# Retention by chunks from block 4 instead of block 8, with values and state as two products in quadrants

## The chip, the cores and the metric

The kernel runs on one core of a Trainium2 chip. The metric is the device time of one execution in microseconds (us), the median over repeated runs. The engines are PE (TensorE, matrix products), DVE (VectorE), ACT (ScalarE), POOL (GpSimd) and SP (SyncE, which here only issues DMAs). Each has its own queue of instructions and works through it in order. They wait for one another through semaphores.

## The reference

The first half is a retention layer, attention without a softmax, in which the weight of a key falls by a factor gamma for each position. The second half is a feed-forward layer with a maximum of three products.

```python
batch, n_heads, seq, head_dim = (8, 8, 576, 64)
scores = scale * np.matmul(q, k.transpose(0, 1, 3, 2))
gamma = 1.0 - 2.0 ** (-5.0 - np.arange(H))
Dmat = np.where(rel >= 0, gamma[:, None, None] ** rel[None, :, :], 0.0)   # rel = query - key
attn = np.matmul(scores * Dmat[None], v)                                  # (8, 8, 576, 64)
x = attn.transpose(0, 2, 1, 3).reshape(4608, 512)
h = np.maximum(np.maximum(x @ w1, x @ w2), x @ w3)                        # w1, w2, w3: 512 x 768
out = h @ w_out                                                           # w_out: 768 x 512
```

q, k and v are fp32. The four weight matrices arrive as float64, and the chip has to turn them into fp32 itself.

## The kernel before

**Tiling.** The 8 x 576 positions are one row of 36 blocks of 128 (`C`), numbered `g`. A sequence is 4.5 blocks long, so it may begin in the middle of a block. `half(c)` is the upper or lower 64 partitions of a tile, and `place(g, c)` says which of the nine half blocks of its sequence a half block is. Nine stages `t` of four blocks each (512 positions, `NT`) go through the feed-forward layer.

**Retention.** The sum over earlier keys is carried as a state, a 64 x 64 matrix for each head: keys (transposed) times values. Blocks 0 to 7 (`g < BY_CHUNKS`) use whole blocks: `transposes` turns keys and queries with PE, and ACT copies them out of PSUM; `scores` multiplies them to 128 x 128 for each head, and DVE multiplies by a causal mask; `state` makes keys times values of the block; `keep` adds it to the state on DVE, and POOL multiplies it by the decay of a block; `values` multiplies values by scores and state by queries; `output` moves the sum into `xT` on DVE, times the query's decay `gq`. In these blocks the values are multiplied by the keys' decay `gk` (POOL, `decay`). Some blocks hold the start of a sequence and use a mask of their own.

From block 8 on, half blocks are used. `chunk_scores` makes, for each head, two score products of 64 x 64 and up to two state products of 64 x 64, on the four quadrants of PE. The tiles `va0` and `va1` hold values in one half of the partitions and the state in the other, and `m0` and `m1` hold masked scores in one half and queries in the other. `chunk_values` then needs one product of full height (128 rows, 64 columns) for each half block and head. For this the queries are copied once on ACT (L313), each half is masked by its own DVE instruction with a mask times key decay, `gm` (L325), and states of a sequence's start are filled with zeros on POOL (L262). The decay `gk` is multiplied into the keys.

**Transposes.** Up to block 6 (`g < BY_PE`) PE transposes. From block 7 on, `load_blocks` brings keys and queries in pieces of 32 x 32, in many small DMAs, and DVE transposes each piece.

**Weights.** `convert_all` makes fp32 out of the float64 words, with DVE and ACT in turn. It works on pairs of 128 rows (`Two`). The first two pairs are done in halves of 512 columns, so that the first half is ready early, all others as 1024 columns at once. `load_weights` issues the next load when a pair is done.

**Feed-forward.** In stage 0 (`up_plain`, `downs_plain`) each of nine units (three pairs of rows times w1, w2, w3) is two times four matmuls of 512 columns, followed by a copy or a maximum (`maximum`). From stage 1 on, `up` and `downs` use products of smaller matrices with sums made beforehand (L766, L564), which needs fewer products.

**The order of the work** is written out by hand. `steps(t)` lists what retention does before each of twelve steps of the previous stage. In stage 0 a step is one unit, and the line `convert(4 if (fp, i) == units[0] else 2)` says how many steps of conversion follow each half unit. DVE's small steps wait in the lists `urgent` and `chores` from stage 1 on and are put between the products; `scaling` is the same for ACT's multiplications by `gk`.

Of the kernel before, what the change touches and what calls it, by code (L numbers as in the profile page):

```python
# [40 lines left out]
FP32 = mybir.dt.float32  # L41
# [11 lines left out]
BY_CHUNKS = 8  # L53
# [28 lines left out]
def kernel(  # L82
# [50 lines left out]
    gq = const.tile([P, 2, NP // 2, C], FP32, name="gq")  # L133
    gm = const.tile([P, H, D], FP32, name="gm")
# [9 lines left out]
                            base=0, channel_multiplier=-1, pattern=[[1, C]])  # L144

# [11 lines left out]
    masks = {0: causal, None: causal}  # L157
    for r in sorted({start_of(g) for g in range(BY_CHUNKS)} - {0, None}):
        m = masks[r] = raw0.tile([C, C], FP32, name=f"causal{r}")
        nc.gpsimd.tensor_copy(m[:], causal[:])  # L160
        nc.gpsimd.memset(m[0:r, r:C], 0.0)


    raws, vds, qks, sts, states, kvs, vas, ms = {}, {}, {}, {}, {}, {}, {}, {}
# [35 lines left out]
    def load_blocks(g, *blocks):  # L200
        for n, src in (("q", q), ("kx", k)):

            if 0 in blocks:
                shape = [P, NP, C // 32, 32] if g < BY_CHUNKS else [P, H, D // 32, 32]
                raws[n, g] = raw.tile(shape, FP32, tag=n, name=n + "raw", bufs=2)
            t = raws[n, g]
            for blk in blocks:
                b, pos = divmod(g * C + 32 * blk, S)
                if g < BY_CHUNKS:
                    for a in range(4):  # L210
                        nc.sync.dma_start(
                            t[32 * a:32 * a + 32, :, blk, :],
                            src[b, a // 2::2, pos:pos + 32, 32 * (a % 2):32 * (a % 2) + 32].rearrange("p j i -> j p i"))
                    continue
                c, e = divmod(blk, 2)
                for a in range(2):
                    r = D * (1 - c) + 32 * a
                    nc.sync.dma_start(
                        t[r:r + 32, :, e, :],
                        src[b, :, pos:pos + 32, 32 * a:32 * a + 32].rearrange("h p i -> p h i"))  # L220

    def stacked(g, c):

        if (g, c) not in vas:
            vas[g, c] = vpool.tile([P, H, D], FP32, tag=f"va{c}", name=f"va{c}")
        return vas[g, c]

    def load(g):
        if g >= BY_PE and ("q", g) not in raws:
            load_blocks(g, *range(C // 32))  # L230
        for n, src in (("k", k), ("q", q), ("v", v)) if g < BY_PE else (("k", k), ("v", v)):
            if n == "v" and g == CPT - 1:
                load_weights(1)
            if n == "v" and g >= BY_CHUNKS:
                for c in range(2):
                    b, pos = divmod(g * C + D * c, S)
                    nc.sync.dma_start(stacked(g, c)[half(c)], v[b, :, pos:pos + D, :].rearrange("h p d -> p h d"))
                continue
            bufs = {"k": 3, "q": 2, "v": 4}[n]
            pool, bufs = (raw0, 1) if n != "v" and g < BY_PE and g % (bufs + 1) == bufs else (raw, bufs)  # L240
            if n == "v":
                t = vpool.tile([C, H, D], FP32, tag="va0", name="vraw")
            else:
                t = pool.tile([C, H, D], FP32, tag=n, name=n + "raw", bufs=bufs)
# [4 lines left out]
    def decay(g):  # L249
        factor = gk[:].unsqueeze(2).to_broadcast([C, H, D])  # L250
        if g < BY_CHUNKS:
            t = vds[g] = vpool.tile([C, H, D], FP32, tag="va1", name="vd")
            nc.gpsimd.tensor_tensor(t[:], raws.pop(("v", g))[:], factor, op=ALU.mult)
            return
        kr = raws["k", g]
        if spread:
            scaling.extend(partial(nc.scalar.mul, kr[:, h, :], kr[:, h, :], gk[:, h:h + 1]) for h in range(H))
        else:
            nc.gpsimd.tensor_tensor(kr[:], kr[:], factor, op=ALU.mult)
        for c in range(2):  # L260
            if place(g, c) == 0:
                nc.gpsimd.memset(vas[g, c][half(1 - c)], 0.0)  # L262
# [4 lines left out]
    def transposes(g):  # L267
        both = qks[g] = {}
        if g >= BY_CHUNKS:
            for n, tag in (("k", "kT"), ("q", "m1")):  # L270
                both[n] = att.tile([P, H, D], FP32, tag=tag, name=tag, bufs=2 if n == "k" else 3)
            ms[g, 1] = both["q"]
        else:
            both["k"] = att.tile([P, NP, C], FP32, tag="kT", name="kT", bufs=2)
            both["q"] = ppool.tile([P, NP, C], FP32, tag="part", name="qT")
        if g >= BY_PE:
# [3 lines left out]
            return  # L280
        for n, src in (("k", raws["k", g]), ("q", raws.pop(("q", g)))):
            pool, tag = (ps_r, "r") if g >= CPT else (ps_x, "x")
            pt = pool.tile([P, NP, C], FP32, tag=tag, name=n + "t")
            for p in range(NP):
                nc.tensor.transpose(pt[:, p, :], pair(src, p), ident[:C, :C])
            nc.scalar.copy(both[n][:], pt[:])

    def scores(g):
# [11 lines left out]
        for j in range(2):  # L300
            st = sts[g, j] = att.tile([C, NP, C], FP32, tag=f"m{j}", name="st", bufs=2 + j)
            soon(partial(nc.vector.tensor_tensor, st[:], s[j][:],
                         masks[start_of(g)][:].unsqueeze(1).to_broadcast([C, NP, C]), op=ALU.mult))

    def begins(g):
        return g + 1 < NG and start_of(g + 1) != 0

    def chunk_scores(g):

        kT, kr = qks[g]["k"], raws.pop(("k", g))  # L310
        sk = [ps_r.tile([P, H, D], FP32, tag="r", name=f"sk{j}") for j in range(2)]
        ms[g, 0] = att.tile([P, H, D], FP32, tag="m0", name="m0", bufs=2)
        nc.scalar.copy(ms[g, 0][half(1)], ms[g, 1][half(1)])  # L313
        for h in range(H):
            for c in range(2):
                if place(g, c) < S // D - 1:
                    nc.tensor.matmul(sk[c][half(c), h, :], lhsT=kr[half(c), h, :], rhs=vas[g, c][half(c), h, :],  # L317
                                     start=True, stop=True)
            for c in (1, 0):
                r = half(1 - c)  # L320
                nc.tensor.matmul(sk[1 - c][half(c), h, :], lhsT=kT[r, h, :], rhs=ms[g, 1][r, h, :],  # L321
                                 start=True, stop=True)

        def mask(c):
            nc.vector.tensor_tensor(ms[g, c][half(c)], sk[1 - c][half(c)], gm[half(c)], op=ALU.mult)  # L325

        def keep_chunk(c):

            to = stacked(g + c, 1 - c)
            if place(g, c) == 0:  # L330
                nc.vector.tensor_copy(to[half(c)], sk[c][half(c)])  # L331
            else:
                nc.vector.tensor_tensor(to[half(c)], sk[c][half(c)], vas[g, c][half(1 - c)], op=ALU.add)  # L333
            if c:
                nc.gpsimd.tensor_tensor(to[half(1)], to[half(1)],  # L335
                                        gs_of[half(1)].unsqueeze(2).to_broadcast([D, H, D]), op=ALU.mult)

        for c in range(2):
            soon(partial(mask, c))
        for c in range(2):  # L340
            if place(g, c) < S // D - 1:
                soon(partial(keep_chunk, c))

    def carry(g):

        for j in range(2):
            nc.scalar.copy(stacked(g, 0)[half(1), j::2, :], states[g][half(j)])

    def state_factors():
        for j in range(2):  # L350
            nc.scalar.copy(gs_of[half(1), j::2], gs[half(j)])

    def key_masks():
        for c in range(2):
            nc.gpsimd.tensor_tensor(gm[half(c)], causal[half(c), half(c)].unsqueeze(1).to_broadcast([D, H, D]),
                                    gk[half(c)].unsqueeze(2).to_broadcast([D, H, D]), op=ALU.mult)

    def state(g):

        kr = raws["k", g]  # L360
        kvs[g] = None
        if begins(g):
            r = start_of(g) or 0
            kvs[g] = ps_r.tile([P, NP, D], FP32, tag="r", name="kv")
            for h in range(H):
                nc.tensor.matmul(kvs[g][half(h % 2), h // 2, :], lhsT=kr[r:, h, :], rhs=vds[g][r:, h, :],
                                 start=True, stop=True)

    def keep(g):
        factor = gs[:].unsqueeze(2).to_broadcast([P, NP, D])  # L370

        def step(t, kv):
            if start_of(g) is not None:
                nc.vector.tensor_tensor(t[:], kv[:], factor, op=ALU.mult)
            else:
                nc.vector.tensor_tensor(t[:], kv[:], states[g][:], op=ALU.add)
                nc.gpsimd.tensor_tensor(t[:], t[:], factor, op=ALU.mult)

        if begins(g):
            t = states[g + 1] = ppool.tile([P, NP, D], FP32, tag="part", name="state")  # L380
            soon(partial(step, t, kvs[g]))
# [7 lines left out]
    def values(chunks, new_states=(), later=False):  # L389

        def before(g):
            return C if start_of(g) is None else start_of(g)

# [5 lines left out]
        pool, tag = (ps_r, "r") if chunks[0] >= CPT - 1 else (ps_y, "y")  # L401
        o = [pool.tile([P, len(chunks), NP // 2, C], FP32, tag=tag, name="o") for _ in range(2)]
        for m, g in enumerate(chunks):
            for n in range(NP):
                for c in range(2):
                    h = head(c, n)
                    nc.tensor.matmul(o[n % 2][half(c), m, n // 2, :], lhsT=vds[g][:, h, :],
                                     rhs=sts[g, h % 2][:, h // 2, :], start=m == 0 and n < 2,
# [604 lines left out]
```

## Time and profile before

| | |
|---|---|
| median of 3 runs | 757.49 us (756.05 to 758.63) |
| profiled run | 756.22 us, span 754.5 us |
| PE matmuls up (L766) | 18% + 15% + 8% + 5% + 5% of the chain that ended last |
| score and state products by chunks (L321, L317) | 896 and 784 records, 220 ns each |
| value products by chunks (L438) | 896 records, 224 ns each |
| masks by chunks on DVE (L325) | 56 of 687 ns, 38.5 us in all |
| copy of the queries on ACT (L313) | 28 of 613 ns, 16.0 us in all |
| multiplication by `gk` on ACT (L186) | 208 of 346 ns, 65.6 us in all |

The profile shows one execution. Busy time is the time in which an engine had at least one instruction in flight; a group's mean is the duration of one instruction, and since matmuls overlap, it isn't what one of them costs. The cost of a stream of matmuls is read from the starts: when the next group of instructions begins. A line is given with the number that it has in this kernel.

### The profile page before, as it was taken

The numbers are of one execution on the slowest core, as the hardware profiler recorded it, in microseconds if no ns is written. First come the engines' busy times: TensorE is split into PE (matmuls) and PEld (weight loads), VectorE is DVE, ScalarE is ACT, GpSimd is POOL, SyncE is SP. The second block draws the span as 40 slices with busy tenths as digits, with TensorE's granted clock in tenths as the row PEclk, the third lists the DMA queues.
The fourth block names the chain that finished last, engine by engine and source line by source line (L and its number), as shares of the span: only waits on it lengthen the run. The fifth ranks groups of instructions, "written<-read, shape, count | busy, mean of one in ns | idle before, by whom it ended". The sixth has DMA issues, their size and how long they took to land.

```text
span 754.5 us, 15014 instructions
## 1 busy us (share of the span) xinstructions
PE 745.1 (99%) x5928; PEld 607.9 (81%) x5928; DVE 529.2 (70%) x879; ACT 336.3 (45%) x670; POOL 90.9 (12%) x112
## 2 busy tenths in 40 slices
PE   8999999999999999999999999999999999999998
PEld 7645545588888888888888888888888888888887
DVE  2998796958886866687567847685768666863662
ACT  3665531155245533553355435542555255414441
POOL 3210012002010110011010102010101010100000
PEclk9999999999999999999999999999999999999999
DMA  9995762504242414242343225242425141000001
GB/s 211 229 244 121 201 140 68 102 1 75 67 101 41 85 43 102 54 74 54 71 85 65 62 60 95 38 77 63 82 40 98 43 91 37 1 30 28 2 1 56
DMA packets 230310, 59.20 MB, mean 78 GB/s; under 512 B 211168, under 2 KB 228960, under 8 KB 230240
## 3 DMA queue, kind: packets, MB, share of 16 engines
q1 hardware_dynamic: 229664, 57.91, 35.5%
q8 instruction: 46, 0.75, 0.4%
q10 hardware_dynamic: 576, 0.33, 0.2%
q14 instruction: 24, 0.20, 0.1%
HBM read 48.76 MB, written 9.44 MB: 77 GB/s over the span
## 4 chain that ended last, share of the span: by engine, by line
PE 89%; DVE 5%; DMA 3%; SPq 1%; issue 1%; ACT 1%; DVEq 0%
PE a L766 18%; PE b L766 15%; PE dx L564 11%; PE c L766 8%; PE up L790 6%; PE dz L564 5%; PE d L766 5%; PE e L766 5%; PE o L438 4%; PE sk L317 3%; PE dy L564 3%; PE down L777 2%; DMA bits<-in_moe_w_out_dram 1%; PE sk L321 1%; SPq L247 1%
## 5 line engine op out<-in xcount | busy, mean ns | idle before, releaser
L754 DVE TENSOR_TENSOR part<-part 128x512 f32<-128x512 f32 x161 | 111.4, 692 | 93.6 <-ACT part L751 91.2
L751 ACT COPY part<-b 128x512 f32<-128x512 f32 x115 | 67.3, 585 | 140.2 <-PE b L766 140.2
L754 DVE TENSOR_TENSOR h<-h,part 128x512 f32<-128x512 f32 x115 | 79.6, 692 | 28.8 <-ACT h L751 24.6
L790 PE MATMUL up<-xT,w 128*128 128x512 f32 (+2 forms) x200 | 84.8, 579 | 1.0 <-DVE w L663 0.9
L751 ACT COPY part<-a 128x512 f32<-128x512 f32 x92 | 53.9, 585 | 48.9 <-PE a L766 48.4
L790 PEld LDWEIGHTS up<-xT,w 128*128 128x128 f32 x200 | 36.8, 190 | 43.3 <-issue 40.1
L766 PE MATMUL a<-s,w 128*128 128x256 f32 x276 | 70.9, 379 | 0.0
L766 PE MATMUL b<-s,n 128*128 128x256 f32 x276 | 70.8, 379 | 0.0
L186 ACT ACTIVATE kraw<-kraw,gk 128x64 f32<-128x64 f32 x208 | 65.6, 346 | 3.2 <-DMA kraw<-in_k_dram 2.9
L766 PEld LDWEIGHTS b<-s,n 128*128 128x128 f32 x276 | 52.4, 190 | 7.1
L766 PEld LDWEIGHTS a<-s,w 128*128 128x128 f32 x276 | 52.4, 190 | 7.2
L534 POOL TENSOR_TENSOR H<-h 128x256 f32<-128x256 f32 x24 | 20.2, 842 | 285.6 <-DVE h L754 285.5
L335 POOL TENSOR_TENSOR va<-va,gs_of 64x512 f32<-64x512 f32 x24 | 25.8, 1074 | 229.8 <-DVE va L333 184.2
L766 PE MATMUL c<-xT,w 128*128 128x256 f32 x184 | 49.1, 389 | 0.0
L766 PE MATMUL d<-s,w 128*128 128x256 f32 x184 | 47.3, 379 | 0.0
L766 PE MATMUL b<-xT,n 128*128 128x256 f32 x184 | 47.2, 379 | 0.0
L564 PE MATMUL dx<-To,H 128*128 128x256 f32 (+1 forms) x204 | 44.9, 370 | 0.0
L766 PE MATMUL e<-xT,w 128*128 128x256 f32 x184 | 43.5, 379 | 0.0
L766 PE MATMUL a<-xT,n 128*128 128x256 f32 x184 | 43.5, 379 | 0.0
L564 PEld LDWEIGHTS dx<-To,H 128*128 128x128 f32 x204 | 36.6, 190 | 4.9
L325 DVE TENSOR_TENSOR m<-sk,gm 64x512 f32<-64x512 f32 x56 | 38.5, 687 | 1.0
L766 PEld LDWEIGHTS e<-xT,w 128*128 128x128 f32 x184 | 35.0, 190 | 5.2 <-DVE va L331 0.2
(122 smaller groups left out, 1318.1 us busy)
## 6 DMA issues: line engine op xcount, KB each, us to landing
bits<-in_moe_w_dram SPq DMA_DIRECT2D x36, 256.0 KB, 5.5
out_dram<-osb SPq DMA_DIRECT2D x35, 256.0 KB, 2.1
kraw<-in_k_dram SPq DMA_DIRECT2D x32, 256.0 KB, 3.1
qraw<-in_q_dram SPq DMA_DIRECT2D x224, 32.0 KB, 2.2
kxraw<-in_k_dram SPq DMA_DIRECT2D x224, 32.0 KB, 2.1
va<-in_v_dram SPq DMA_DIRECT2D x56, 128.0 KB, 3.1
bits<-in_moe_w_out_dram SPq DMA_DIRECT2D x6, 512.0 KB, 6.3
vraw<-in_v_dram SPq DMA_DIRECT2D x7, 256.0 KB, 4.5
```

The source lines that it names most:

```text
L186: scaling.popleft()()
L317: nc.tensor.matmul(sk[c][half(c), h, :], lhsT=kr[half(c), h, :], rhs=vas[g, c][half(c), h, :], start=True, stop=True)
L325: nc.vector.tensor_tensor(ms[g, c][half(c)], sk[1 - c][half(c)], gm[half(c)], op=ALU.mult)
L335: nc.gpsimd.tensor_tensor(to[half(1)], to[half(1)], gs_of[half(1)].unsqueeze(2).to_broadcast([D, H, D]), op=ALU.mult)
L438: nc.tensor.matmul(o[half(c), n % 2, n // 2, half(m)], lhsT=vas[g, m][:, h, :], rhs=ms[g, m][:, h, :], start=m == 0 and n == 0, stop=True, ...
L534: urgent.append(lambda: (pool(s3, a11, a21, op=ALU.subtract), pool(s4, a12, s2, op=ALU.subtract)))
L564: nc.tensor.matmul(o, lhsT=hS[n](fp)[:, m * P:(m + 1) * P], rhs=late["T"][n][:, fp, cols], start=first and fp == order[0] and (m == 0 or l ...
L751: nc.scalar.copy(of[step], ps[step[0]][:])
L754: nc.vector.tensor_tensor(of[dst], a, b, op=op)
L766: nc.tensor.matmul(ps[chain][:, e, :], lhsT=factor(w, 2 * fp + e), rhs=xS[t][x], start=n == 1 and e == 0, stop=ends, skip_group_check=True)
L777: nc.tensor.matmul(b[:], lhsT=h[:, fb, m * P:(m + 1) * P], rhs=w_sb["out", fb], start=(fb == 0), stop=(fb == NF - 1))
L790: nc.tensor.matmul(ps[:, cols], lhsT=w_sb[i, fb][:, dc * P:(dc + 1) * P], rhs=xT[t][:, dc, cols], start=dc == 0 and cols.start == 0, stop= ...
```

## The change

`BY_CHUNKS` falls from 8 to 4, so blocks 4 to 7 are done by chunks too. The form of the work by chunks changes:

- `chunk_scores` makes scores (`sk`) and new states (`kv`) in one PSUM tile each, and masks with one DVE instruction for a block.
- Values and state are two products, each on quadrants of 64 x 64: `chunk_values` first multiplies values by masked scores, then the state by the queries, into the same two PSUM tiles for two blocks. For the first half block of a sequence the second product is left out.
- The decay `gk` is multiplied into the values, no longer into the keys. The mask `low` is then only ones and zeros.
- Values are loaded as a whole block. States have tiles of their own (`stacks`).
- `transposes` for blocks 4 to 6 puts PE's result in the layout by chunks with eight ACT copies of 64 partitions in place of two of 128.
- Gone are the tiles `gm` and `m0`'s copy of the queries, the zero fills, and the masks for blocks in which a sequence starts.
- In the conversion the third pair of weights is done in halves too. In stage 0 the second unit gets as many conversion steps as the first, and for the last unit the maximum is put ahead of the conversion.

```diff
-BY_CHUNKS = 8
+BY_CHUNKS = 4
...
     def decay(g):
         factor = gk[:].unsqueeze(2).to_broadcast([C, H, D])
...
+        t = raws.pop(("v", g))
+        if spread:
+            vds[g] = t
+            scaling.extend(partial(nc.scalar.mul, t[:, h, :], t[:, h, :], gk[:, h:h + 1]) for h in range(H))
             return
...
+        vds[g] = t if g >= BY_CHUNKS else vpool.tile([C, H, D], FP32, tag="s", name="vd")
+        nc.gpsimd.tensor_tensor(vds[g][:], t[:], factor, op=ALU.mult)
...
     def transposes(g):
...
+        if g >= BY_CHUNKS:
+            for n, pt in pts:
+                for j in range(2):
+                    for c in range(2):
+                        nc.scalar.copy(both[n][half(c), j::2, :], pt[half(j), :, half(c)])
...
     def chunk_scores(g):
...
-        sk = [ps_r.tile([P, H, D], FP32, tag="r", name=f"sk{j}") for j in range(2)]
-        ms[g, 0] = att.tile([P, H, D], FP32, tag="m0", name="m0", bufs=2)
-        nc.scalar.copy(ms[g, 0][half(1)], ms[g, 1][half(1)])
+        s, kv = (ps_r.tile([P, H, D], FP32, tag="r", name=n) for n in ("sk", "kv"))
+        kept = [c for c in range(2) if place(g, c) < S // D - 1]
         for h in range(H):
             for c in range(2):
-                if place(g, c) < S // D - 1:
-                    nc.tensor.matmul(sk[c][half(c), h, :], lhsT=kr[half(c), h, :], rhs=vas[g, c][half(c), h, :],
-                                     start=True, stop=True)
-            for c in (1, 0):
-                r = half(1 - c)
-                nc.tensor.matmul(sk[1 - c][half(c), h, :], lhsT=kT[r, h, :], rhs=ms[g, 1][r, h, :],
+                nc.tensor.matmul(s[half(c), h, :], lhsT=kT[half(c), h, :], rhs=qT[half(c), h, :],
                                  start=True, stop=True)
-
-        def mask(c):
-            nc.vector.tensor_tensor(ms[g, c][half(c)], sk[1 - c][half(c)], gm[half(c)], op=ALU.mult)
+            for c in kept:
+                nc.tensor.matmul(kv[half(1 - c), h, :], lhsT=kr[half(c), h, :], rhs=vd[half(c), h, :],
+                                 start=True, stop=True)
+
+        def mask():
+            nc.vector.tensor_tensor(st[:], s[:], low[:, 0:D].unsqueeze(1).to_broadcast([P, H, D]), op=ALU.mult)
...
     def chunk_values(chunks, t, i):
-        outs = [ps_r.tile([P, 2, NP // 2, C], FP32, tag="r", name="o") for _ in chunks]
-        for g, o in zip(chunks, outs):
-            for m in range(2):
-                for n in range(NP):
-                    for c in range(2):
-                        h = head(c, n)
-                        nc.tensor.matmul(o[half(c), n % 2, n // 2, half(m)], lhsT=vas[g, m][:, h, :],
-                                         rhs=ms[g, m][:, h, :], start=m == 0 and n == 0, stop=True,
-                                         skip_group_check=True)
+        o = [ps_r.tile([P, 2, NP, D], FP32, tag="r", name="o") for _ in range(2)]
+        cross = ((0, 0), (1, 1), (0, 1), (1, 0))
+        for n, g in enumerate(chunks):
+            for u in range(NP):
+                for m, c in cross:
+                    h = head(c, u)
+                    nc.tensor.matmul(o[m][half(c), n, u, :], lhsT=vds[g][half(m), h, :], rhs=sts[g][half(m), h, :],
+                                     start=n == 0 and u == 0, stop=place(g, m) == 0, skip_group_check=True)
+        for n, g in enumerate(chunks):
+            for u in range(NP):
+                for m, c in cross:
+                    h = head(c, u)
+                    if place(g, m) > 0:
+                        nc.tensor.matmul(o[m][half(c), n, u, :], lhsT=stacks[g][half(m), h, :],
+                                         rhs=qks[g]["q"][half(m), h, :], start=False, stop=True, skip_group_check=True)
...
-        two = Two(2)
+        two = Two(3)
         two.exponent(both)
...
-                    convert(4 if (fp, i) == units[0] else 2)
+                    if (fp, i) == units[-1]:
+                        maximum()
+                        convert(2)
+                        continue
+                    convert(4 if (fp, i) in units[:2] else 2)
                     maximum()
```

The hand-written order of steps keeps its places. In stage 1's list the carry of the state into chunk form moves from block 8's turn to block 4's, and the whole-block state steps fall away.

## The prediction

> **What bounds the kernel now.** I read the page's busy times and slices first, then a table of windows by stage, the PE waits, and the PE and ACT timelines of the one stage where the table shows slack.
>
> ```profile
> span 754.5 us, 15014 instructions
> ...
> PE 745.1 (99%) x5928; PEld 607.9 (81%) x5928; DVE 529.2 (70%) x879; ACT 336.3 (45%) x670; POOL 90.9 (12%) x112
> ...
> DVE  2998796958886866687567847685768666863662
> ACT  3665531155245533553355435542555255414441
> ```
>
> PE is busy all the time, but DVE is at nine tenths early on (a slice is 18.9 us). The windows, with their columns (length, then busy time and count of PE, PEld, DVE, ACT, POOL, then clock, DMA share, GB/s), split this:
>
> ```profile
> 25.00:60.00 35.00, 33.97 (x148) 17.66 (x140) 32.62 (x46) 23.77 (x29) 4.36 (x4) 1.00 1.03 231
> ...
> 180.00:740.00 560.00, 560.00 (x4620) 490.99 (x4619) 387.94 (x649) 255.10 (x549) 60.59 (x71) 1.00 0.28 59
> ```
>
> From 180 us on PE has no idle time, and the list of PE waits over that stretch is empty. There, only fewer PE nanoseconds make the kernel faster; relief of DVE, ACT, POOL or DMA is worth nothing. Before 60 us DVE is busy 32.62 of 35 us and PE can be made to wait:
>
> ```profile
> 28.93 0.60 PE L285 MATMUL kt<-ident,kraw 128*128 128x128 f32 x4
> 29.37 0.60 PE L285 MATMUL qt<-ident,qraw 128*128 128x128 f32 x4
> 29.81 3.60 PE L790 MATMUL up<-xT,w 128*128 128x512 f32 x8
> 33.34 1.16 PE L299 MATMUL s<-qT,kT 64*128 64x128 f32 x16
> ...
> 43.94 7.13 PE L790 MATMUL up<-xT,w 128*128 128x512 f32 x16 [0.89 <-DVE w L663]
> ```
>
> Block 4 is transposed at 29 us and scored at 33.34; the third pair of weights (w3, DVE product L663) comes 0.9 us late at 43.94, with 1.05 us between the last transpose's own time and that start. ACT evacuates the transposes:
>
> ```profile
> 30.76 0.72 ACT L648 ACTIVATE expo<-expo,inf 128x512 int32<-128x512 f32 x1
> 31.39 0.57 ACT L795 COPY h<-up 128x512 f32<-128x512 f32 x1
> 31.86 0.59 ACT L286 COPY kT<-kt 128x512 f32<-128x512 f32 x1
> 32.33 0.60 ACT L286 COPY qT<-qt 128x512 f32<-128x512 f32 x1
> 32.81 0.78 ACT L639 ACTIVATE mant<-bits,one 128x512 f32<-128x512 uint32 x1
> ```
>
> The copies end at 32.93, 0.4 us before PE wants them. This is the tightest spot that the change touches.
>
> Last, the rate of small products, a score block and a value block:
>
> ```profile
> 214.81 0.23 PE L317 MATMUL sk<-va,kraw 64*64 64x64 f32 x2
> 214.82 0.23 PE L321 MATMUL sk<-m,kT 64*64 64x64 f32 x2
> 214.87 0.23 PE L317 MATMUL sk<-va,kraw 64*64 64x64 f32 x2
> 214.88 0.22 PE L321 MATMUL sk<-m,kT 64*64 64x64 f32 x2
> ...
> 234.19 2.08 PE L438 MATMUL o<-m,va 128*64 128x64 f32 x64
> ```
>
> Each fp32 matmul leaves two records. Four records on four quadrants start within 20 ns, and the next four follow 58 ns after (214.81 to 214.87). A value block of two blocks has 64 records in 2.02 us to the next start (236.21): 32 pairs at 58 ns plus 0.2 us on entering and leaving.
>
> **What the skill says.** "TensorE: Matmul & The Clock Gate", Part 3 (Packing small matmuls), has tiles of the array run concurrently, starts about 4 ns apart; the trace has 6 to 7 ns. "TensorEngine Tiling (Array Packing)", Key Properties, says that a change of tiling mode drains PE; the 0.2 us at the block's two ends agrees. "PSUM — Partial Sum Buffer", PSUM bank collisions, quotes a vendor rule that two row tiles may not use one bank at once, and reports a measured error only within one bank and one group of 32 partitions. The kernel before always gives a row tile its own bank, so its trace shows nothing on this. "ScalarE: Activation LUTs", Rules for kernel authors, has 0.83 ns per element; the copies (585 ns for 512 columns, 372 for 256) agree.
>
> **The change part by part.**
>
> *Steady part, blocks 8 to 35.* Scores keep their count and quadrant order: 0. Values: 64 full-height records for two blocks become 128 quadrant records, 32 groups of four at 58 ns instead of 32 pairs at 58 ns: 0, within 0.1 us for each of 14 blocks. Of DVE go 28 masks (56 at 687 ns become 28 at the same), of ACT 28 copies at 613 ns (17 us); no PE wait stands behind either. Decay by ACT moves from keys to values, 208 at 346 ns either way. Values are issued up to 2 us after keys on SP's queue; ACT waited for keys at two places (2.9 us in all), and behind it stand PSUM copies for PE. I take 0; bound 0 to +2.
>
> *Blocks 4 to 7 on PE.* Removed, from the PE timeline: scores 1.09 + 1.09 + 1.99, values 1.80 + 1.80, states 0.61 + 1.03 + 0.56, state times query 0.83 + 1.03: 11.8 us. Added: four score blocks by chunks, half of 2.02 each with up to 0.1 more for a block alone, 4.2, and two value blocks of 2.02: 8.2. Gain 3.6.
>
> *Transposes of blocks 4 to 6.* Two ACT copies each become eight of 256 columns. Nearest rows: 372 ns from PSUM, 404 ns for the carry's strided copies; back to back 0.27 to 0.41 apart, I take 0.30. For block 4, ACT frees at 31.39; two carry copies (0.8), the h copy (0.5), then copies from 32.7 to 35.2; the sixth, with which PE can start, ends at 34.6. PE wants them at 33.37: **a new wait of 1.3 us** (1.1 to 2.2). Behind the copies on ACT stands the conversion of w2's second half, done at 37.15 instead of 34.95; DVE idles for it, and w3 behind it.
>
> *Third pair narrow.* DVE wide: 0.6 + 0.8 + 1.15 + 1.26 + 1.14 = 5.0 us; narrow: twice about 2.6, so +0.3, but the first half is ready early. w2's second half is ready at 38.6; two steps of 0.34, mask and state 1.3, two of 0.34, then 0.6 + 0.6 + 0.7: w3's first half at 43.1. PE: scores end at 35.8, w2 6.97, transposes 0.87: it asks at 43.65. The wait of 1.05 goes.
>
> *DVE until the fifth unit.* Block 5: one mask and two states at 0.7 for two masks at 0.6, +0.9. With the 2.2 us lost behind ACT, w1's second pair is ready at 51.8 (asked at 51.8), and w2's second pair, 8.3 us of DVE work later, at 60.1, where PE asks at 58.9: **a wait of 1.2** (0 to 2.3).
>
> *After that* PE has 7 us a unit and DVE about 6. SP's issues matter until 107 us, 0.49 us each whatever the size: block 7 needs 16 instead of 32, so weights of the later units come 5 us sooner. The masks and states of blocks 6 and 7 (six at 0.7 for four at 0.6, +1.8) stand before the first output weights, ready at 100.2 where PE asks at 100.0: 0.25. The wait of 0.48 at 103.42 for the last maximum goes, as it is now put ahead of a conversion. The wait of 1.1 us at 174.9 for block 11's transposes stays: the same DVE instructions stand ahead of it. POOL loses the masks and key masks (2.6 us before 10 us) and six memsets, which nobody waits for. ACT issues two more DMAs of out_decay before 10 us (0.7 us each), in slack.
>
> *Sum.* PE work -3.6; waits removed -1.05 - 0.48; added +1.3 + 1.2 + 0.25, and 0.5 for block 5's copies and w1's second pair, which come with no slack: **-1.8 us** of a span of 754.5. Bounds: slow copies and the DVE loss behind them give -0.9, fast ones -2.7. The profiled run measured 756.22, the three runs 756.05 to 758.63, median 757.49; I take the sum from the median: 755.7, and 754.8 to 756.6 as this case's own range.
>
> **Rivals.** *All gain.* If the copies and DVE keep up, the waits fall away: -3.6 - 1.05 - 0.48, and -1.1 if block 11's wait goes too: 751.3 to 752.4. For it: every wait is under 2 us, and SP's relief feeds DVE sooner. Against: DVE's 32.62 of 35. *A new bound in conversion.* With copies at 0.41 or more, a raw pair released late, or values late behind ACT, waits of 4 to 7 us: 757 to 760. *Banks (slower).* The score block puts two row tiles into one bank, in sk and in kv. If they serialize, a group of four takes up to 111 ns instead of 58. There are 16 groups in each of 32 blocks, 512: +27 us at full price, 784; at half, 769. It decides from about 8 ns a group (1.8 + 2.3 over 512). Against it: the skill's measured case. *The change doesn't do what it says:* the instruction lists of the two kernels show 512 score, 448 state, 512 and 456 value products, so it does; what it may not do is shorten PE's stream in the steady part.
>
> **How the numbers follow.** About 0.3% (2.3 us) is what a measurement can tell from no change. Likeliest case 0.54, almost all of it within 0.3%, with a fourth below by the run's own scatter; all gain 0.24; conversion 0.13, half within; banks 0.09. Faster: 0.24 + 0.17, rounded to 0.41; same 0.39; slower 0.20. The range leaves out most of the banks case: 751.3 to 760.5.
>
> **What would show it.** Right: score and value blocks of 2.0 us for two blocks; PE waiting about 1.3 us for ACT's copies near 33 us; w3 without a wait; PE without waits from 180 us on. Wrong: groups in score blocks well over 58 ns (banks); a value block away from 2.0 us; PE waits over 3 us in all between 25 and 125 us, or none.

## The result and the profile after

The changed kernel takes 765.92 us (median of 4 runs, 765.21 to 766.33), the kernel before 758.02 in the same comparison (756.05 to 758.63): a ratio of 1.0108, 95% interval 1.0087 to 1.0129. It is slower; the forecast was 755.7 in 751.3 to 760.5. One sentence of the description ahead of the prediction is wrong: the order of steps does not keep its places. In stage 2's list, `s = m + 2 if first_pair else m + 1` became `s = m + 2 if t == 2 else m + 1`, so blocks 10 and 11 are scored one step later, and block 12 is transposed one step later.

The head of the page (busy us, share of the span, instructions):

```profile
span 764.0 us, 17021 instructions
...
PE 748.3 (98%) x6952; PEld 608.5 (80%) x6952; DVE 513.6 (67%) x855; ACT 325.5 (43%) x663; POOL 84.5 (11%) x101
...
DVE  2899897757876874677576756676567656763662
```

DVE, ACT and POOL all do less than before and PE's busy time is 3.2 us longer, in a span 9.5 us longer. The list of PE's waits (what PE waited for, us in total, times, longest):

```profile
PE up L754 <- DVE w L626: 3.2, 2, 1.7
PE sk L296 <- DVE qT L188: 2.1, 1, 2.1
PE down L741 <- DVE w_out L626: 1.9, 1, 1.9
PE warm L153 <- POOL ident masks.py:199: 1.4, 1, 1.4
PE sk L296 <- ACT qT L265: 1.1, 1, 1.1
PE s L278 <- ACT qT L260: 0.9, 1, 0.9
PE dx L527 <- DVE H L496: 0.9, 1, 0.9
```

The wait for w2's second pair (1.7, the larger of the first row), the one for block 12's queries (2.1), for the output weights (1.9), for block 4's copies (1.1) and for H (0.9) are new. The windows shown for the kernel before, now for the changed one (length, busy and count of PE, PEld, DVE, ACT, POOL, then clock, DMA share, GB/s):

```profile
25.00:60.00 35.00, 33.07 (x197) 17.26 (x198) 30.98 (x48) 26.51 (x43) 4.13 (x4) 0.95 0.99 229
180.00:740.00 560.00, 556.42 (x5453) 486.97 (x5452) 366.18 (x619) 239.13 (x520) 55.21 (x63) 1.00 0.29 59
```

PE now idles 1.9 of the 35 us early on (1.0 before) and 3.6 us after 180 us (none before), and the clock is below 1.00 in the first. Finer windows show where, in pairs of a stretch with a wait and the one behind it:

```profile
34.10:37.50 3.40, 2.53 (x49) 1.83 (x50) 1.08 (x2) 3.25 (x8) 0.00 (x0) 1.00 1.12 240
37.50:40.90 3.40, 3.40 (x5) 1.35 (x4) 2.70 (x6) 2.20 (x4) 0.00 (x0) 0.50 1.22 258
102.40:105.70 3.30, 1.39 (x4) 0.48 (x3) 3.27 (x4) 2.70 (x3) 0.00 (x0) 1.00 0.59 115
105.70:109.10 3.40, 3.40 (x5) 1.35 (x4) 3.30 (x5) 1.51 (x2) 0.00 (x0) 0.51 0.36 80
218.40:221.80 3.40, 1.31 (x8) 0.80 (x7) 2.16 (x5) 1.35 (x3) 0.00 (x0) 1.00 0.00 0
221.80:225.20 3.40, 3.40 (x111) 3.40 (x112) 2.48 (x4) 0.00 (x0) 0.00 (x0) 0.50 0.31 50
```

Three times PE gets half its clock for 3.413 us right after a wait, so 1.7 us of work is left undone; the kernel before has no such stretch but at its end. In them a 512-column matmul takes 0.85 us in place of 0.43, and the score block at 221.8 takes 3.62 us in place of 2.02.

The form itself runs at the rate that was forecast. A value block of two blocks in the steady part:

```profile
281.62 1.16 PE L395 MATMUL o<-m,vraw 64*64 64x64 f32 x64
282.60 1.11 PE L402 MATMUL o<-qT,s 64*64 64x64 f32 x64
283.65 1.56 PE L527 MATMUL dx<-To,H 128*128 128x256 f32 x6
```

281.62 to 283.65 is 2.03 us, as for the full-height form. To see where time goes, the starts of the feed-forward matmuls, which both kernels issue in the same order, are set against each other. The difference of the two starts is called the lag here; a growing lag is time lost. The lag of the changed kernel grows or shrinks so (us; place by the kernel before's time):

| place | change of lag | what it is |
|---|---|---|
| first unit, 25.4 | +0.35 | first weights |
| block 4's scores, 35.0 | +1.59 | wait 1.08, slower block, fewer products |
| 36 to 38 | +1.68 | half clock |
| w3, 43.9 | -1.05 | its wait is gone |
| w2's second pair, 59.1 | +1.75 | wait |
| values of blocks 4 and 5, 69.7 | -1.54 | PE work saved |
| first output weights, 100.3 | +2.21 | wait |
| 101 to 103 | +1.80 | half clock |
| last maximum, 103.4 | -0.49 | its wait is gone |
| values of blocks 6 and 7, 118.1 | -1.48 | PE work saved |
| stage 2, 180 to 233 | +4.38 | waits, half clock |
| 374 | +0.44 | a small wait |

The lag is 4.84 us when stage 0 ends and 9.6 at the end of the feed-forward matmuls.

### The profile page after: what moved, and what is told of

It reads as the page before. It is cut to its first block, busy times and chain, and to the rows that moved or that the text cites. A ratio compares the mean times of both kernels' runs of the same rounds, so it can differ in the third digit from the quotient of the medians.

```text
span 764.0 us, 17021 instructions
## 1 busy us (share of the span) xinstructions
PE 748.3 (98%) x6952; PEld 608.5 (80%) x6952; DVE 513.6 (67%) x855; ACT 325.5 (43%) x663; POOL 84.5 (11%) x101
## 4 chain that ended last, share of the span: by engine, by line
PE 88%; DMA 5%; DVE 4%; SPq 2%; issue 1%; ACT 0%; POOL 0%; DVEq 0%; ACTq 0%; POOLq 0%
PE a L730 18%; PE b L730 15%; PE dx L527 11%; PE c L730 8%; PE up L754 6%; PE dz L527 5%; PE e L730 5%; PE d L730 5%; PE sk L296 3%; PE down L741 3%; PE dy L527 2%; PE o L395 2%; PE o L402 2%; DMA bits<-in_moe_w_dram 2%; DMA kraw<-in_k_dram 2%; SPq L225 1%
## 5 line engine op out<-in xcount | busy, mean ns | idle before, releaser
L754 PE MATMUL up<-xT,w 128*128 128x512 f32 (+2 forms) x200 | 86.7, 588 | 3.2 <-DVE w L626 3.2
L183 ACT ACTIVATE vraw<-vraw,gk 128x64 f32<-128x64 f32 x208 | 65.3, 346 | 3.0 <-DMA vraw<-in_v_dram 2.9
L313 POOL TENSOR_TENSOR s<-s,gs_of 64x512 f32<-64x512 f32 x24 | 25.7, 1072 | 253.9 <-DVE s L311 252.3
L296 PEld LDWEIGHTS sk<-qT,kT 64*64 64x64 f32 x1024 | 33.2, 140 | 11.2 <-issue 5.5
L730 PEld LDWEIGHTS a<-xT,n 128*128 128x128 f32 x184 | 34.9, 190 | 5.5 <-ACT part L715 0.8
```

What stands on the lines that cost most here:

```text
L183: scaling.popleft()()
L296: nc.tensor.matmul(s[half(c), h, :], lhsT=kT[half(c), h, :], rhs=qT[half(c), h, :], start=True, stop=True)
L313: nc.gpsimd.tensor_tensor(new, new, factor, op=ALU.mult)
L730: nc.tensor.matmul(ps[chain][:, e, :], lhsT=factor(w, 2 * fp + e), rhs=xS[t][x], start=n == 1 and e == 0, stop=ends, skip_group_check=True)
L754: nc.tensor.matmul(ps[:, cols], lhsT=w_sb[i, fb][:, dc * P:(dc + 1) * P], rhs=xT[t][:, dc, cols], start=dc == 0 and cols.start == 0, stop= ...
```

## The experiments

The ratios are all to the kernel before, with 95% intervals. The kernel before was measured again beside each group of kernels: its median was 758.02 us beside the changed kernel, 756.05 beside e1 to e4, 757.02 beside e5 to e8 and 756.16 beside e9 to e11. So a difference of medians between two groups can be off by 2 us; where it matters, the difference by ratios is given too. The theory was: the form costs nothing, and the loss is in waits of stage 0 and in the moved step. The rivals: the quadrants or shared banks, and the conversion's new pacing.

**The moved step.**

```diff
-            s = m + 2 if t == 2 else m + 1
+            s = m + 2 if a == 2 * CPT else m + 1
```

> The changed kernel with one line of the order of work put back: blocks 10 and 11 are scored one step earlier again, and with them block 12 is transposed one step earlier. Theory (the moved step made block 12's transposes late): the PE wait of 2.1 us at 222 us and the stretch at half clock behind it (1.6 us) go, block 11's wait of 1.3 us comes back: 2 to 4 us less than the changed kernel, about 763. Rival (quadrants or shared PSUM banks cost time all along): no change, 766.

Measured: 760.98 us, ratio 1.0055 (1.0039 to 1.0071): 4.9 us less than the changed kernel by medians, 4.0 by ratios, the upper end of what was expected. The lag of 4.3 us at the end of stage 0 hardly grows through stage 2 (4.8 us at the end). How one step costs so much shows in the changed kernel's DVE timeline:

```profile
218.16 0.70 DVE L188 STREAM_TRANSPOSE kT<-kxraw 128x512 f32<-128x512 f32 x1
218.79 0.38 DVE L437 TENSOR_TENSOR w<-w,w 128x256 f32<-128x256 f32 x1
220.41 0.69 DVE L718 TENSOR_TENSOR h<-h,part 128x512 f32<-128x512 f32 x1 [1.24 <-ACT h L715]
221.02 0.70 DVE L188 STREAM_TRANSPOSE qT<-qraw 128x512 f32<-128x512 f32 x1
221.65 0.67 DVE L188 STREAM_TRANSPOSE kT<-kxraw 128x512 f32<-128x512 f32 x1
```

Block 12's queries are transposed at 221.02, behind an addition that waits 1.24 us for ACT, while PE has asked for them since 219.7. In the kernel before the same transpose starts at 212.58, and PE's scores without a wait:

```profile
214.70 0.27 PE L317 MATMUL sk<-va,kraw 64*64 64x64 f32 x2
```

The transposes also set free the buffers of the next loads. SP's timeline, and then ACT's, of the changed kernel (the value in brackets is idle time and what ended it):

```profile
221.75 4.78 SPq L208 DMA_DIRECT2D qraw<-in_q_dram  x8
226.57 3.90 SPq L208 DMA_DIRECT2D kxraw<-in_k_dram  x8
230.57 0.40 SPq L225 DMA_DIRECT2D kraw<-in_k_dram  x1
231.07 0.53 SPq L225 DMA_DIRECT2D vraw<-in_v_dram  x1
```

```profile
234.67 0.35 ACT L183 ACTIVATE vraw<-vraw,gk 128x64 f32<-128x64 f32 x1 [2.29 <-DMA vraw<-in_v_dram]
234.93 0.57 ACT L715 COPY part<-a 128x512 f32<-128x512 f32 x1
```

SP issues 18 loads for a later block from 221.75 on; its values, last in the row, land 3.6 us after their issue at 231.07. ACT stands 2.29 us at the multiplication by `gk`, with a PSUM copy behind it that PE waits for (0.39 us on the PE timeline, at 235.54). In e1_steps_back SP's row begins at 214.35, and neither wait is there. The 2.1 us, the half clock, the 0.9 us for H and this one are all of the one moved line.

**ACT's eight copies.**

```diff
-            for p in range(NP):
-                nc.tensor.transpose(pt[:, p, :], pair(src, p), ident[:C, :C])
...
+            for h in range(H):
+                for c in range(2):
+                    nc.tensor.matmul(pt[half(c), h, :], lhsT=src[half(c), h, :], rhs=ident[half(c), half(c)],
+                                     start=True, stop=True)
+            nc.scalar.copy(both[n][:], pt)
```

> The changed kernel, but PE transposes blocks 4 to 6 head by head on the two diagonal quadrants, so that the result has the layout by chunks already and ACT needs one copy of 512 columns in place of four of 256. Theory (ACT's eight copies make the wait at block 4's scores and, behind them, delay w2's second half): the wait of 1.1 us at 36 us and the half clock behind it (1.7 us) go, and 1 us more by the earlier conversion: 3 to 4 us less than the changed kernel, about 762.5. Rival (the conversion's new pacing makes the loss in stage 0): at most 1 us less.

Measured: 764.87 us, ratio 1.0114 (1.0098 to 1.0131): 1.1 us less by medians, nothing by ratios. The theory's mechanism is there. The wait at block 4 and its half clock went (the lag at 35.0 is 0.09 us in place of 1.94), DVE waits 0.29 us in place of 2.32 for ACT behind the copies, and w2's second pair is used at 61.28 us in place of 63.39 (1.0 of these 2.1 us come from an earlier first unit). But the edit pays for this itself: 32 products on two quadrants cost PE 1.23 us more for each of the three blocks, 3.7 us in all, and the waits for w2's second pair (1.8) and for the output weights (2.0) are as long as in the changed kernel (1.7 and 1.9). So this run doesn't show what the wait alone is worth.

**The clock.** For the three waits, idle products ahead of the first real one, into the same PSUM tile (here block 4: 6, block 12: 10; likewise 10 at the first output product):

```diff
+        for _ in range({CPT: 6, 3 * CPT: 10}.get(g, 0)):
+            nc.tensor.matmul(s[:, 0:2, :].rearrange("p h d -> p (h d)"), lhsT=ident[:], rhs=ident[:], start=True, stop=True)
```

> The changed kernel with idle products (128 columns, result overwritten) on PE ahead of block 4's scores (6), block 12's scores (10) and the first output product (10), so that PE is busy in the three waits that were followed by half clock; the waits themselves stay. Theory (the clock falls because PE stood idle): the three stretches at half clock go, 1.6 us each, about 5 us less than the changed kernel, 761. Rival (the clock falls on its own, or because of load): the stretches stay, and the time with them, 766 or up to 1 us more.

Measured: 764.95 us, ratio 1.0119 (1.01 to 1.0139): 1.0 us less by medians and nothing by ratios, not 5. All three stretches are at full clock, so the half clock does come from the idling. But the 1.7 us won at 37.5 were waited away at block 5's scores (+1.26) and at w2's second pair (+2.13 for +1.75), where a new stretch at half clock followed (64.8 us), and what was won at 222 was waited away at 235, for the same late values (PE idles 2.5 us there). So the three stretches do not add up to a cost of 5 us: the ones at 37.5 and 222 cost nothing, since PE then waits for data that come no earlier. The new stretch at 64.8 does cost: the lag at 69.7 is 4.76 us in place of 2.80, and the wait for the output weights behind it is no shorter (+2.29 for +2.21). There DVE keeps step with PE: in the changed kernel it stands 0.81 us for PE at 94.26, ahead of its work for the output weights.

**The conversion.** Undone in the changed kernel, and done alone in the kernel before:

```diff
-        for n in (1, 2):
+        for n in (1,):
...
-                    if (fp, i) == units[-1]:
...
-                    convert(4 if (fp, i) in units[:2] else 2)
+                    convert(4 if (fp, i) == units[0] else 2)
```

> The changed kernel with the three edits of the weights' conversion undone: third pair as 1024 columns at once, two conversion steps in the second unit, no maximum put ahead in the last unit. Theory (the narrow pair pays for itself): w3's wait of 1 us comes back and little else moves, 0 to 2 us more than the changed kernel, 766 to 768. Rival (the new pacing costs the time in stage 0): 3 to 6 us less, 760 to 763.

> The kernel before with only the three edits of the conversion. Theory (DVE has room for them when blocks 4 to 7 are whole): w3's wait of 1 us and the wait of 0.4 us for the last maximum go, 0 to 1.5 us less than the kernel before, 755 to 757. Rival (the narrow pair delays the conversion): w2's second pair or the output weights come late, 1 to 4 us more than before.

Measured: 763.55 us without the edits, ratio 1.0104 (1.0083 to 1.0125), 2.4 us less by medians, against my expectation, but only 0.3 by ratios; 756.79 us with them alone, ratio 0.9998 (0.9989 to 1.0006). The first is no proof for the rival: its trace has one stretch at half clock in place of three, since its waits of 1.5 and 2.1 us fall otherwise (see the last experiment). The second settles it: alone the edits cost and bring nothing that can be measured. The wait for w3 goes (-1.05), but +0.46 at w2's second pair and +0.64 at the output weights give it back.

**The form alone.** The kernel before with quadrants, one mask and the decay on values from block 8 on (`chunk_scores`, `chunk_values`, `decay`, `carry`, the loads and the layout of `gq` as in the changed kernel, `BY_CHUNKS = 8`).

> The kernel before with the new form by chunks from block 8 on, and nothing else of the change: blocks 4 to 7, the conversion and the order of work as before. Theory (the form costs nothing on PE, as the block times of 2.02 us say): within 1.5 us of the kernel before, 755 to 758, with score and value blocks of 2.02 us. Rival (shared banks or the later landing of values cost time in every stage): 760 or more.

Measured: 757.58 us, ratio 1.0003 (0.9991 to 1.0015), with blocks of 2.02 us. From 180 us on:

```profile
180.00:740.00 560.00, 560.00 (x5372) 491.19 (x5372) 368.64 (x624) 240.61 (x524) 55.02 (x63) 1.00 0.28 59
```

PE has no idle time, as before. DVE does 19.3 us and ACT 14.5 us less than in the kernel before (387.94 and 255.10), for no gain. So shared banks and late values are out, and the loss lies in blocks 4 to 7 and the moved step.

**POOL beside DVE.** In the changed kernel, ahead of the first output weights, DVE and then POOL:

```profile
98.70 1.41 DVE L311 TENSOR_TENSOR s<-kv,s 64x512 f32<-64x512 f32 x2 [0.49 <-POOL s L313]
100.14 0.69 DVE L758 TENSOR_TENSOR h<-h,up 128x512 f32<-128x512 f32 x1
100.75 2.12 DVE L600 TENSOR_SCALAR expo<-bits 128x1024 int32<-128x1024 int32 x1
102.79 1.21 DVE L618 SCALAR_TENSOR_TENSOR expo<-bits,expo 128x1024 int32<-128x1024 int32 x1
104.04 1.23 DVE L626 TENSOR_TENSOR w_out<-mant,expo 128x1024 f32<-128x1024 f32 x1
```

```profile
100.28 1.04 POOL L313 TENSOR_TENSOR s<-s,gs_of 64x512 f32<-64x512 f32 x1 [1.61 <-DMA kxraw<-in_k_dram]
101.28 1.04 POOL L235 TENSOR_TENSOR vraw<-vraw,gk 128x512 f32<-128x512 f32 x1
```

The same work in the kernel before, from the last masks to the product:

```profile
94.47 2.48 DVE L198 TENSOR_TENSOR st<-s,causal 128x512 f32<-128x512 f32 x4
96.87 0.68 DVE L637 TENSOR_SCALAR expo<-bits 128x1024 int32<-128x1024 int32 x1
97.47 1.22 DVE L655 SCALAR_TENSOR_TENSOR expo<-bits,expo 128x1024 int32<-128x1024 int32 x1
98.72 1.22 DVE L663 TENSOR_TENSOR w_out<-mant,expo 128x1024 f32<-128x1024 f32 x1
```

An instruction that takes 0.68 us there takes 2.12 in the changed kernel: it starts while POOL multiplies, and ends 0.55 us after POOL's second instruction (102.32). The same happens at 59.30 (2.07 for 1.22), 61.40 (1.95 for 1.22) and 82.11 (1.95 for 1.23): 3.7 us in all, and 0.5 of waiting for POOL. The Trainium skill, "SBUF — State Buffer", Who interferes with whom, says this: DVE and POOL share a pair of ports as an exclusive lock, for DVE instructions with two inputs in SBUF and for those in its two-port modes, and the loser blocks fully. The numbers agree. The next kernel is e1_steps_back with POOL kept out of the rest of stage 0 (only block 5's decay stays on it):

```diff
-                if c:
-                    nc.gpsimd.tensor_tensor(new, new, factor, op=ALU.mult)
+                if c and g >= 2 * CPT:
+                    nc.gpsimd.tensor_tensor(new, new, factor, op=ALU.mult)
+                elif c and g % 2:
+                    for h in range(H):
+                        nc.scalar.mul(new[:, h, :], new[:, h, :], gs_of[r, h:h + 1])
+                elif c:
+                    nc.vector.tensor_tensor(new, new, factor, op=ALU.mult)
...
+        if g > CPT + 1:
+            vds[g] = t
+            for h in range(H):
+                nc.scalar.mul(t[:, h, :], t[:, h, :], gk[:, h:h + 1])
+            return
```

> e1_steps_back with POOL kept out of stage 0 from block 4 on: the states of blocks 5 and 7 are multiplied by their decay on ACT, those of 4 and 6 on DVE, and the values of blocks 6 to 8 on ACT. Theory (the conversion on DVE is late because DVE's instructions take up to three times as long while POOL multiplies: 1.6 us lost ahead of w2's second pair, 2.2 us and a wait of 0.5 us ahead of the first output weights): both PE waits shrink to under 1 us in all and the half clock at 105 us goes, 3 to 5 us less than e1_steps_back, 756 to 758. Rival (DVE is late by the number of its instructions alone): 0 to 1 us more than e1_steps_back, since DVE and ACT get more to do.

Measured: 757.03 us, ratio 1.0 (0.9989 to 1.0011): 4.0 us less than e1_steps_back (4.2 by ratios) and level with the kernel before. By ratios, the moved step and POOL make up the whole loss, 4.0 + 4.2 of 8.2 us. Its DVE timeline at the same place:

```profile
98.46 0.69 DVE L768 TENSOR_TENSOR h<-h,up 128x512 f32<-128x512 f32 x1
99.06 0.69 DVE L610 TENSOR_SCALAR expo<-bits 128x1024 int32<-128x1024 int32 x1
99.67 1.22 DVE L628 SCALAR_TENSOR_TENSOR expo<-bits,expo 128x1024 int32<-128x1024 int32 x1
100.92 1.23 DVE L636 TENSOR_TENSOR w_out<-mant,expo 128x1024 f32<-128x1024 f32 x1
```

and two of its PE waits:

```profile
PE down L751 <- DVE w_out L636: 0.6, 1, 0.6
PE up L764 <- DVE w L636: 0.4, 1, 0.4
```

The output product starts at 102.20 in place of 105.32, no stretch is at half clock, and the lag at the end of stage 0 is 0.03 us. Yet PE still does 3 us less work in blocks 4 to 7 (-1.54 and -1.48), and w3's wait is gone (-0.93): against them stand +1.73 at block 4's scores, +1.26 at block 5's, +0.56 at w2 and +0.53 at the output weights with the last maximum. These take the whole gain.

**All together, and what is left.** The three edits in one kernel; then e5_pool_clear with `(carry, a)` moved from step 0 to step 2; then this with the conversion undone.

> The edits of e1_steps_back, e2_quad_tr and e5_pool_clear together. Theory: the gain of 3.2 us in blocks 4 to 7 is left, less about 1 us of small waits: 754 to 756, at or a little under the kernel before. Rival (a new bound on DVE or ACT takes over): 758 to 761.

> e5_pool_clear with the carry of the state into chunk form (two ACT copies, 0.8 us, needed only by the values of block 4) moved from ahead of block 4's ACT copies to behind its scores. Theory (ACT's queue sets the start of block 4's scores): the wait of 1.2 us shrinks by 0.7 to 0.8, and the time by as much: about 756.3, just under the kernel before. Rival (DVE, which makes the weights, sets the pace of stage 0): w2's second pair and the output weights are awaited longer by the same amount, 757.0 again.

> e9_carry_late with the three conversion edits undone as in e4_conv_back. Theory (four conversion steps in the second unit put ACT steps that wait for DVE ahead of block 5's eight copies, so that its score block takes 2.1 us in place of 1.0): that 1.1 us goes, w3's wait of 1 us comes back: within 0.5 us of e9_carry_late. Rival (the edits as a whole cost time): 1 us less or more.

Measured: e6_combined 756.67, ratio 0.9994 (0.9986 to 1.0002); e9_carry_late 756.17, 1.0002 (0.9993 to 1.0011); e10_carry_conv 756.95, 1.0007 (1.0 to 1.0015). None beats the kernel before. The carry's move took 0.9 us off what the lag grows by at 35.0 (+0.85 for +1.73), and w2's second pair took 0.6 of it back (+1.20 for +0.56). The median is the one that the theory named, but the kernel before stood at 756.16 beside it, and the ratio hasn't moved. So the rival holds for most of the 0.9 us; whether the rest is kept, the runs can't tell. In e10_carry_conv block 5's score block is quick again, so the second unit's four conversion steps, which wait for DVE on ACT's queue, do delay its copies; but w3's wait came back (+1.21 for -1.05), with half clock behind it.

**Waits of known length.** In the kernel before, at 36 points of stages 3 to 8:

```diff
+    def stall(n):
+        ps = ps_r.tile([P, P], FP32, tag="r", name="stall")
+        nc.tensor.matmul(ps[:], lhsT=ident[:], rhs=ident[:], start=True, stop=True)
+        nc.scalar.copy(scr[:], ps[:, 0:64])
+        for _ in range(n):
+            nc.scalar.copy(scr[:], scr[:])
+        ps = ps_r.tile([P, P], FP32, tag="r", name="stall")
+        nc.tensor.matmul(ps[0:64], lhsT=scr[:], rhs=ident[:], start=True, stop=True)
```

> The kernel before with artificial waits of PE in stages 3 to 8, each a chain of one to six small ACT copies between two idle products, so that PE idles for about 1 to 4 us at many points. No part of the reference's work is left out. Theory (the clock is set for stretches of 3.413 us on a fixed grid, by how long PE idled in the stretch before, and 1.8 to 1.9 us of idling is the limit): stretches at half clock start on one grid, and follow stretches with more than about 1.9 us of idling and no others. Rival (a wait of a given length always lowers the clock, wherever it falls): half clock follows the longer waits whatever their place on the grid.

Measured: 827.98 us. The waits came out at 0.30 to 1.74 us, shorter than meant. Three stretches at half clock begin at 352.7, 714.6 and 799.9 us, 106 and 25 times 3.413 us apart, so there is a grid of such stretches. Four grid stretches hold a whole wait of 1.74 us; three of them were followed by half clock, and none of the others, which idle 1.69 us or less (two of the 1.74 us waits lie across a boundary). Over the other kernels whose records show the grid, stretches with 1.91 to 2.10 us of idling were followed by half clock seven times of seven, and those with 1.69 to 1.81 never; two with 0.91 and 1.21 us were, and these hold block 4's small products, but a third such stretch with 1.30 us (e5_pool_clear) was not. So, these two apart, the limit is near half of a stretch, 1.7 to 1.9 us. Both theory and rival were partly right: length decides, but only what of it lies in one stretch. Why the two fell stays open. The Trainium skill, "TensorE: Matmul & The Clock Gate", Part 1, What's actually happening, has the free-running window of 3413 ns, which agrees, and puts the fall after one idle window; here half a window was enough.

## Why the prediction was wrong

**Right.** *Steady part*: taken at 0, and 0 (the form alone). *Blocks 4 to 7 on PE*: 3.6 forecast, 3.0 at the value blocks, where most of it is seen. w3's wait and the last maximum's went as said. The *banks* rival was rightly held unlikely (its full price is 783 us by the prediction's own terms, not 784). The sign of being wrong that was named came: between 25 and 125 us PE waits 6.2 us in all (3.2 + 1.9 + 1.1).

**"A new wait of 1.3 us" at block 4.** The mechanism was right. Four copies take 1.50 us, 0.38 each, not 0.30:

```profile
31.70 0.81 ACT L327 COPY s<-state 64x256 f32<-64x256 f32 x2
32.42 0.57 ACT L759 COPY h<-up 128x512 f32<-128x512 f32 x1
32.90 1.50 ACT L265 COPY kT<-kt 64x256 f32<-64x256 f32 x4
34.42 1.54 ACT L265 COPY qT<-qt 64x256 f32<-64x256 f32 x4
```

The score block starts at 34.84 after 1.08 us, and then takes 2.14 us in place of 1.02, as it meets the last copies one by one: 2.2 us in all, the upper bound given.

**"A wait of 1.2 (0 to 2.3)" for w2** was 1.7: in its bounds, but only in part by its cause. The loss on DVE behind ACT's copies is there (2.32 us of idling at 36.80). But POOL's lock costs 0.85 and 0.73 us on the two DVE instructions just ahead, and without POOL 0.4 is left (e5_pool_clear).

**"The masks and states of blocks 6 and 7 ... 0.25"** is the first step that failed. The wait is 1.9 us, the lag grows by 2.21, and 1.8 of half clock came with it. The sum counted 0.7 us for each state on DVE and put POOL's part at nothing. Here DVE loses 1.43 us on the instruction at 100.75 and waits 0.49 for POOL: with the 0.25 that makes 2.17. From block 4 to the end of stage 0 POOL doesn't have much more to do: three state multiplications of 1.04 to 1.46 us in place of two of 0.61 and 0.93, and as many decays. But two of the three (58.83 and 100.28) now stand right ahead of a decay, beside DVE's conversion. The kernel before has one such DVE instruction, 1.64 us at 71.92 in place of 1.22, which I passed over.

**"The wait of 1.1 us at 174.9 for block 11's transposes stays: the same DVE instructions stand ahead of it"** is the second. The condition of `s` was not compared; blocks 10 and 11 moved a step, that wait went, and 4 to 5 us came in its place (e1_steps_back). With it fell "PE without waits from 180 us on".

**"0.5 for block 5's copies and w1's second pair"** was too small. Where half clock hasn't made PE late already, block 5's scores alone add 1.26 to the lag (e1_steps_back, e5_pool_clear). The 0.8 us more here and the 0.9 more at block 4 (2.2 for 1.3) are about what e5_pool_clear, without POOL and the moved step, lacks: it is level with the kernel before, and not 1.8 us under it.

**No rival had these.** "A new bound in conversion" named waits of 4 to 7 us and 757 to 760; that is what e1_steps_back, without the moved step, comes near to (760.98). Half clock behind a wait was not priced anywhere. Of the changed kernel's three stretches only the one at 105.7, with no wait of PE's behind it for long, cost its 1.8 us in full.

## What to carry to other kernels

POOL's work beside a DVE that PE waits for is paid on DVE: price it at up to POOL's duration, not at nothing, and look at where it falls. Compare every condition in an order of work, not only its list, and follow a moved step to the buffers that it sets free and the loads that stand behind them. PE time saved ahead of data that come no earlier is lost in the wait for them, as the 1.7 us at 37.5 were; where the other engine keeps step with PE, as behind 64.8, it is not. A price for a wait needs to say which of the two holds.

## What the runs showed of the hardware

- Half clock for 3.413 us followed a stretch of the 3.413 us grid in which PE idled 1.91 to 2.10 us (seven of seven) or held a whole wait of 1.74 us (three of four). It did not follow 1.69 to 1.81 us in the other kernels (three of three), nor a wait of 1.74 us that lay across a boundary (two of two). Two stretches with 0.91 and 1.21 us and small products are exceptions.
- Two products of 64 x 64 on the two diagonal quadrants took as long as four on all four: transposing a block's keys and queries by 32 of them takes 2.0 us (28.72 to 30.73 in e6_combined), 0.13 us for two, and a score block of 64 products 2.02 us, 0.13 us for four. Eight transposes of 128 columns take 0.88 us (28.81 to 29.69 in e5_pool_clear).
- Two row tiles in one PSUM bank, on different partitions, ran as fast as in banks of their own: 2.02 us for the score products of two blocks in e7_form_only, as in the kernel before.
